# An mLSTM cell and a hash-routed expert layer on one core: moving two experts' weight loads to SyncE, a first layer into the attention block, and sums and turns into other gaps

## The chip, the core and the metric

The kernel runs on one core of a Trainium2 chip. A core has TensorE (matrix products into PSUM), VectorE, ScalarE and GpSimd (element work; GpSimd does not read PSUM here), and SyncE, which in this kernel only issues loads and stores. Loads and stores are also issued by ScalarE and, where rows are picked by an index, by GpSimd. Each engine works through its own list of instructions in order; semaphores tie the lists together.

The metric is the device time of one execution in microseconds. Before the change it is 373.84 us, the median of 3 runs (373.79 to 373.99).

## The reference, cut to what matters

Two blocks follow each other. The first is a recurrent attention cell over 4 batches, 8 heads and 768 positions, with heads of 40:

```python
for t in range(S):
    m_new = np.maximum(f_gate[:, :, t] + m, i_gate[:, :, t])
    f_stab = np.exp(f_gate[:, :, t] + m - m_new)
    i_stab = np.exp(i_gate[:, :, t] - m_new)
    m = m_new
    C = f_stab[:, :, None, None] * C + i_stab[:, :, None, None] * np.einsum('bhd,bhe->bhde', vt, kt)
    n = f_stab[:, :, None] * n + i_stab[:, :, None] * kt
    h_tilde = np.einsum('bhde,bhe->bhd', C, qt)
    denom = np.maximum(np.abs(np.einsum('bhd,bhd->bh', n, qt)[:, :, None]), 1.0)
    y[:, :, t] = o * h_tilde / denom          # o = sigmoid(o_gate[:, :, t])
```

Its output, laid out as 3072 rows of 320, is the input of the second block: eight experts, each a two-layer network with a ReLU. The expert of a row is a hash of its token id, so a row's expert is known from `token_ids` alone:

```python
expert_idx = token_ids * np.int64(2654435761) % np.int64(E)      # E = 8
for e in range(E):
    mask = expert_idx == e
    h = np.maximum(x[mask] @ w1[e], 0.0)                         # w1: 8 x 320 x 1024
    out[mask] = h @ w2[e]                                        # w2: 8 x 1024 x 320
```

Everything is float32. One expert's weights are 1.31 MB for `w1` and 1.31 MB for `w2`.

## The kernel before, in words

**Attention block.** The rows are cut into 24 tiles of 128 positions (`NT`), four batches by six stretches. A loop over s from 0 to 23 writes out by hand, instruction by instruction, the order of the work: the whole block stands in a manual schedule, so each engine executes in the order of the code, with small deviations. In step s TensorE turns the keys and queries of tile s+2 (`turn`, L332), forms the scores of tile s+1 (L380) and its decay matrices (L343, L351), and attends for tile s (L432, L438). VectorE weighs the scores (L386), divides (L447 to L451) and does small pieces of two side tasks: the gates' sums and splits (`Gates`, the object `g2` serves the last stretch), and the routing. GpSimd multiplies with the output gate (`gated`, L455), and SyncE stores the finished tile's rows to `x_rows` in DRAM (L458).

The routing turns token ids into two index tables: `g_idx` says which row of `x_rows` goes to which slot of which expert, `s_idx` where the result row goes. Its pieces are spread over the steps by the dictionaries `pieces` (VectorE and GpSimd) and `products` (TensorE, at a step's end): one-hot matrices in eight parts (`route_hot`), four table products (`route_table`), then `route_index` and `route_tiles`. The products' PSUM tiles bear the tag of the turns (`tr`, two banks).

During the last steps the weights of expert 0 come in slices over SyncE (`slices_of`), and two of its three full row tiles, whose rows all lie in the first 19 tiles, are gathered and turned (`early_turn`).

**Expert block.** An expert has three full tiles of 128 slots and a rest of 32 (`CAP` 416 slots); the rests of four experts make one further tile (`rest`, L1099). For experts 1 to 7 both layers use a seven-product scheme for 2x2 blocks (Strassen's, in Winograd's form): `layer1_by_seven` (L951, L959) needs sums of the rows (`sums_of_x`, L912 to L915, tile `tx`) and of the first weights (`sums_of_w1`, L905 to L908, tile `sw`); `layer2_by_seven` (L1022) needs sums of h and differences of the second weights. It works in two halves of 208 columns by two row-block pairs each: seven products into four PSUM banks, VectorE additions out of them (L937), ScalarE ReLUs. The banks of the first half are those of the second, so TensorE's second product of the second half waits for VectorE's addition out of the first half's second bank. The third full tile of each expert goes through plain `layer2` (L990). Results leave by a copy into `zo` (L835) and an indexed store (L839, GpSimd).

Rows come to an expert in four steps. `fetch(e)` lets GpSimd gather three tiles by `g_idx` (L110), and SyncE writes them to a DRAM buffer `x_slots` (L1068; the rests L1075). `blocks(e)` reads them back as twelve small loads into `xb`, with 32x32 blocks in place (L1083, SyncE). `turned(e)` turns the blocks in one VectorE instruction (L1087). Expert 0 is an exception: `layer1` first runs over its two early tiles (columns 0 to 256), then `layer2` over them, and the third tile and the rest are gathered and turned by TensorE in between (`turns0`, L852 to L858).

Weights of experts 1 and 2 are issued by ScalarE from inside expert 0's first `layer1` (the argument `between`): L97, L100 twice, L101. Those of expert e+3 are issued by SyncE at the end of expert e.

In the loop over e, expert e+2's rows are fetched, and expert e+1's are turned and summed, after expert e's `layer2` and before its `layer2_by_seven`:

```python
            layer2(W[e], h, (2,), cols_of(s_idx, e * NJ), True)
            if e + 1 < E:
                if e + 2 < E:
                    fetch(e + 2)
                    blocks(e + 2)
                turned(e + 1)
                sw = sums_of_w1(W[e + 1])
                tx = sums_of_x(xTs[e + 1])
            if i == EG - 1:
                rest(g)
            if e > 0:
                layer2_by_seven(W[e], tw, h, sh, cols_of(s_idx, e * NJ))
            if e + 3 < E:
                load_weights(e + 3)
```

**Semaphores of loads.** The framework gives the loads of SyncE and ScalarE eight completion semaphores in turn. Before a load is issued its engine waits until the previous load on the same semaphore has landed.

Of the kernel before, what the change touches and what calls it, by code (L numbers as in the profile page):

```python
# [17 lines left out]
P = 128  # L18
# [4 lines left out]
def kernel(  # L23
# [96 lines left out]
    def slices_of(e):  # L120
# [17 lines left out]

        return [lambda i=i: part(i) for i in range(7)]

    firsts = (0, 1, NB - 1, NB)
# [10 lines left out]
    with tc.tile_pool(name="gates", bufs=1) as gp, \  # L152
# [304 lines left out]
        def store(s):  # L457
            nc.sync.dma_start(x_d[s * P : (s + 1) * P, :], st.pop(s)["x"].rearrange("p h d -> p (h d)"))  # L458
# [52 lines left out]
        def route_turned():  # L511
            tp = ps.tile([P, NT], F32, name="tpe", tag="tr", bufs=2)
            nc.tensor.transpose(tp[:], et[:], ident[:NT, :NT])
            nc.vector.tensor_copy(ef[:], tp[:])
# [222 lines left out]
        for s in range(NT):  # L737
# [121 lines left out]

    def layer1(w, xT, h, c0, c1, between=lambda fp: None):  # L860

        w1t, w1c, _ = w
        for fp in range(FB // 2):
            hp = [mps.tile([P, CAP], F32, name="mh", bufs=4) for _ in range(2)]

            def halves(first):
                for i in range(2):
                    r = slice(i * P // 2, (i + 1) * P // 2)
                    nc.tensor.matmul(  # L869
                        hp[i][:, : c1 - c0], lhsT=w1c[r, fp, :], rhs=xT[r, 2, c0:c1], start=first, stop=not first,  # L870
                    )

            def whole(i, first):
                fb = 2 * fp + i
                for db in range(2):
                    nc.tensor.matmul(
                        hp[i][:, : c1 - c0], lhsT=w1t[:, db, fb * P : (fb + 1) * P], rhs=xT[:, db, c0:c1],
                        start=(first and db == 0), stop=(not first and db == 1),
                    )

            def out(i):
                if i == 0:
                    nc.vector.tensor_relu(h[:, 2 * fp, c0:c1], hp[i][:, : c1 - c0])
                else:
                    nc.scalar.activation(h[:, 2 * fp + 1, c0:c1], hp[i][:, : c1 - c0], AF.Relu)  # L885

            if fp % 2 == 0:
                for i in range(2):
                    whole(i, True)
                between(fp)  # L890
                halves(False)
                for i in range(2):
                    out(i)
            else:
                halves(True)
                for i in range(2):
                    whole(i, False)
                    out(i)
                between(fp)

# [30 lines left out]
    def layer1_by_seven(w, sw, xT, tx, h, done):  # L931

# [9 lines left out]
        for g in range(0, FB // 2, 2):  # L942
# [112 lines left out]
    with tc.manual_schedule():  # L1055
# [50 lines left out]
        fetch(1)  # L1106
        blocks(1)
        for e in range(E):
            g, i = e // EG, e % EG
            h = xp.tile([P, FB, CAP], F32, name="h", bufs=1) if e else h0  # L1110
            if i == 0:
                hrem[g] = xp.tile([P, EG, FB, RM], F32, name="hrem")

            if e == 0:
                layer1(W[0], xT0, h, 0, 2 * P, lambda fp: len(W) < 3 and load_weights(len(W), nc.scalar))
                layer2(W[0], h, range(2), cols_of(s_idx, 0), True, lambda j: j == 0 and turns0())
            if e == 0:
                layer1(W[e], xT0, h, 2 * P, CAP)
            else:
                tw = differences_of_w2(W[e])  # L1120
                sh = xp.tile([P, 4, FB // 2, P], F32, name="sh", bufs=1)
                layer1_by_seven(
                    W[e], sw, xTs[e], tx, h,
                    lambda g: sums_of_h(h, sh, g, nc.vector if g else nc.gpsimd),
                )
            nc.gpsimd.tensor_copy(hrem[g][:, i], h[:, :, NM:])
            layer2(W[e], h, (2,), cols_of(s_idx, e * NJ), True)
            if e + 1 < E:
                if e + 2 < E:
                    fetch(e + 2)  # L1130
                    blocks(e + 2)
                turned(e + 1)
                sw = sums_of_w1(W[e + 1])
                tx = sums_of_x(xTs[e + 1])
            if i == EG - 1:
                rest(g)
            if e > 0:
                layer2_by_seven(W[e], tw, h, sh, cols_of(s_idx, e * NJ))
            if e + 3 < E:
                load_weights(e + 3)  # L1140

    nx = nc.values_load(xe[0:1, NX : NX + 1], min_val=0, max_val=NX)
    with tc.If(nx > 0):
        with tc.For_i(0, nx, 1) as k:
# [9 lines left out]
            xT = xp.tile([P, DB, CAP], F32, name="xT")  # L1154
            h = xp.tile([P, FB, CAP], F32, name="h", bufs=1)
            gather(xr[:, :Dm], gs[:, 0:1])
            turn(xr, xT[:, :, :P], False)
            layer1(w, xT, h, 0, P)
            layer2(w, h, range(1), lambda j: gs[:, 1:2], False)

# [29 lines left out]
```

## Time and profile before

| | |
|---|---|
| median of 3 runs | 373.84 us |
| profiled execution, its own time | 374.24 us |
| its span, first to last instruction | 372.1 us |
| TensorE, VectorE, GpSimd, ScalarE busy | 93%, 58%, 56%, 37% of the span |
| mean granted TensorE clock | 0.984 |
| last product of attention ends, about | 132.4 us |
| layer one of expert 1 starts | 174.4 us |
| layer one of expert 2 starts | 201.3 us |

The profile is a record of one execution. Start times are microseconds from the span's start. PE is TensorE, DVE VectorE, ACT ScalarE, POOL GpSimd; SPq and ACTq are the loads that SyncE and ScalarE issue, with the time of the issue, not of the transfer. `x_slots<-xg` means that `x_slots` is written from `xg`. A tail in square brackets is how long the engine was idle before the instruction and what ended that. The view of waits sums such idle times by pair: total, times, longest. The chain is followed back from the last instruction, at each step to what released it. Numbers behind an L are lines of the kernel before.

### The profile page before, as it was taken

What the parts mean: (1) busy time and instruction counts of PE and PEld (TensorE: products, weight loads), DVE (VectorE), ACT (ScalarE), POOL (GpSimd) and SP (SyncE); (2) the same over time, 40 slices, a digit from 0 to 9 for tenths busy, and PEclk for the clock granted to TensorE, in tenths of its full rate; (3) what the DMA queues carried; (4) which work ended last, traced back from release to release, by engine and by line L of the source; (5) the groups of instructions that cost most, each with busy time, mean ns of one, the idle gap of its engine ahead of it and who ended that gap; (6) DMA issues with size and microseconds to landing.
All of it is one profiled execution on the core that took longest, in us unless ns stands there. A gap on an engine that the chain in (4) does not pass through costs nothing.

```text
span 372.1 us, 9193 instructions
## 1 busy us (share of the span) xinstructions
PE 344.4 (93%) x3595; PEld 295.1 (79%) x3595; DVE 215.4 (58%) x494; ACT 138.1 (37%) x311; POOL 206.9 (56%) x292
## 2 busy tenths in 40 slices
PE   7899899999999987399998999999999999999990
PEld 7777788878888764278988889859989899899680
DVE  7567787798779731017566483563483574755310
ACT  6476578666666530011320312301312313212210
POOL 8432668898883415021964936843936747419312
PEclk9999999999999999699999999999999999999997
DMA  7699989989898889560378695495945865200000
GB/s 145 120 182 174 185 164 197 211 173 202 171 201 221 212 259 333 191 132 3 124 161 281 140 303 147 83 296 166 235 139 153 199 192 135 36 18 35 9 11 36
DMA packets 163155, 59.35 MB, mean 159 GB/s; under 512 B 140130, under 2 KB 159102, under 8 KB 163110
## 3 DMA queue, kind: packets, MB, share of 16 engines
q1 hardware_dynamic: 155606, 44.97, 53.2%
q0 software_dynamic: 2496, 8.20, 7.1%
q10 hardware_dynamic: 5008, 5.57, 4.8%
q8 instruction: 29, 0.48, 0.5%
q14 instruction: 16, 0.13, 0.1%
HBM read 46.57 MB, written 12.48 MB: 159 GB/s over the span
## 4 chain that ended last, share of the span: by engine, by line
PE 75%; DVE 8%; DMA 7%; issue 4%; ACT 2%; POOL 2%; SPq 1%; ACTq 0%; DVEq 0%; POOLq 0%
PE mh L951 17%; PE mh L1022 11%; PE zp L990 10%; PE sp L380 7%; PE tr L332 6%; PE mh L959 5%; PE xh L438 4%; PE ab L343 3%; PE xh L432 3%; PE zp L1099 2%; PE xh L411 2%; DMA xr<-x_rows,g_idx 2%; DMA x_rows<-x 2%; SPq L1083 1%; DVE w L386 1%
## 5 line engine op out<-in xcount | busy, mean ns | idle before, releaser
L839 POOL DMA_INDIRECT out_dram<-zo,s_idx x26 | 26.2, 1006 | 83.3 <-ACT zo L835 49.0
L990 PE MATMUL zp<-w2t,h 128*128 128x320 f32 x160 | 46.7, 445 | 7.5 <-ACT h L885 7.5
L990 PEld LDWEIGHTS zp<-w2t,h 128*128 128x128 f32 x160 | 30.9, 196 | 19.5 <-ACT h L885 8.0
L937 DVE TENSOR_TENSOR h<-u,mh 128x416 f32<-128x416 f32 x42 | 24.6, 588 | 30.2 <-PE mh L959 13.9
L438 PE MATMUL xh<-v,w 128*64 128x41 f32 x768 | 34.9, 222 | 0.3 <-issue 0.3
L386 DVE TENSOR_TENSOR w<-sp,w 128x512 f32<-128x512 f32 x48 | 30.7, 682 | 4.8 <-ACT w L347 4.8
L347 ACT ACTIVATE w<-ab 128x512 f32<-128x512 f32 x48 | 26.1, 597 | 17.1 <-PE ab L343 17.0
L110 POOL DMA_INDIRECT xg<-x_rows,g_idx x24 | 24.5, 1019 | 14.0 <-PE mh L869 7.0
L951 PE MATMUL mh<-tx,sw 128*128 128x208 f32 x168 | 31.8, 339 | 0.0
L438 PEld LDWEIGHTS xh<-v,w 128*64 128x64 f32 x768 | 30.7, 138 | 0.4 <-issue 0.4
L380 PE MATMUL sp<-qT,kT 64*128 64x128 f32 x384 | 29.3, 285 | 1.5 <-DVE w L386 1.2
L951 PEld LDWEIGHTS mh<-tx,sw 128*128 128x128 f32 x168 | 29.7, 190 | 0.0
L380 PEld LDWEIGHTS sp<-qT,kT 64*128 64x128 f32 x384 | 24.3, 187 | 6.0 <-issue 2.3
L1022 PE MATMUL mh<-tw,sh 128*128 128x160 f32 x168 | 27.4, 299 | 0.0
L432 PE MATMUL xh<-C,qs 128*64 128x82 f32 x320 | 27.3, 249 | 0.0
L455 POOL TENSOR_TENSOR x<-x,og 128x320 f32<-128x320 f32 x24 | 20.6, 863 | 10.7 <-ACT og L372 6.9
L421 POOL TENSOR_TENSOR C<-C,add 64x164 f32<-64x164 f32 x32 | 16.3, 509 | 14.8 <-ACT add L415 13.6
L1022 PEld LDWEIGHTS mh<-tw,sh 128*128 128x128 f32 x168 | 24.3, 190 | 0.0
L951 PE MATMUL mh<-xT,w1t 128*128 128x208 f32 x112 | 24.3, 339 | 0.0
L937 DVE TENSOR_TENSOR u<-m,mh 128x416 f32<-128x416 f32 x28 | 15.9, 587 | 14.2 <-ACT m L965 7.1
L959 PE MATMUL mh<-xT,w1c 64*128 64x208 f32 x224 | 23.5, 349 | 0.0
L974 ACT ACTIVATE h<-mh 128x416 f32<-128x416 f32 x14 | 7.2, 517 | 42.6 <-PE mh L959 39.3
(236 smaller groups left out, 744.5 us busy)
## 6 DMA issues: line engine op xcount, KB each, us to landing
w2t<-in_moe_w_dram SPq DMA_DIRECT2D x5, 1280.0 KB
w1t<-in_moe_w_dram SPq DMA_DIRECT2D x5, 1024.0 KB
xb<-x_slots SPq DMA_DIRECT2D x84, 52.0 KB
k<-in_k_dram SPq DMA_DIRECT2D x24, 160.0 KB
v<-in_v_dram SPq DMA_DIRECT2D x24, 160.0 KB
og<-in_o_gate_dram SPq DMA_DIRECT2D x24, 160.0 KB
x_rows<-x SPq DMA_DIRECT2D x24, 160.0 KB
q<-in_q_dram SPq DMA_DIRECT2D x23, 160.0 KB
```

The costliest lines, as they stand in the source:

```text
L110: nc.gpsimd.indirect_dma_start(out=xg, out_offset=None, in_=x_d[:rows, :], in_offset=bass.IndirectOffsetOnAxis(ap=idx, axis=0),)
L347: nc.scalar.activation(w[:, hf], ab[:], AF.Exp)
L380: nc.tensor.matmul(sp[hf][:, j, :], lhsT=d["kT"][r, j, :], rhs=d["qT"][r, j, :], start=True, stop=True)
L386: nc.vector.tensor_tensor(d["w"][:, hf], d["sp"][hf][:], d["w"][:, hf], op=ALU.mult)
L432: nc.tensor.matmul(xh[t, 2 * j : 2 * j + 2, :], lhsT=d["qs"][:, j, t], rhs=Cs[b][c % 2][:, j].rearrange("p h d -> p (h d)"), start=True, s ...
L438: nc.tensor.matmul(hs[t, 2 * j + hf, :], lhsT=d["w"][:, hf, j, t], rhs=d["v"][:, 2 * j + hf, :], start=(c == 0), stop=True, skip_group_che ...
L839: ins = nc.gpsimd.indirect_dma_start(out=out[:, :], out_offset=bass.IndirectOffsetOnAxis(ap=idx, axis=0), in_=zo[:], in_offset=None, bound ...
L937: nc.vector.tensor_tensor(o, a, b, op=ALU.add)
L951: nc.tensor.matmul(pair(bank[n])[:, a], lhsT=lhsT(g + a), rhs=rhs, start=first and a == 0, stop=True, skip_group_check=True,)
L959: nc.tensor.matmul(pair(bank[n])[:, a], lhsT=w1c[k, g + a, :], rhs=xT[k, 2, r], start=False, stop=True, skip_group_check=True,)
L990: nc.tensor.matmul(zp[:], lhsT=h[:, fb, j * P : (j + 1) * P], rhs=w[2][:, fb, :], start=(fb == 0), stop=(fb == FB - 1),)
L1022: nc.tensor.matmul(bank[n], lhsT=lhsT(f), rhs=rhs(f), start=first and f == 0, stop=f == FB // 2 - 1, skip_group_check=True,)
```

## The change

The change has these parts.

1. **Weights of experts 1 and 2.** ScalarE no longer issues them. SyncE does, after expert 1's `fetch` and `blocks` and before expert 2's.
2. **First layer's first part.** `layer1` is moved up and takes its PSUM banks as an argument. Its run over expert 0's first 256 columns now stands at the end of the attention block, on banks of the turns and decays (`tr`, `ab`).
3. **Fetch.** `fetch(e + 2)` and `blocks(e + 2)` stand at the head of expert e.
4. **Turns and sums.** `turned(e + 1)` is called inside expert e's `layer1_by_seven`, in the first half, behind its first three VectorE additions, and `sums_of_x` likewise in the second half (`meanwhile`). For expert 1 both stand after expert 0's second `layer1`. `tx` gets two buffers. `sums_of_w1` stays.
5. **h.** All experts use the one buffer `h0`.
6. **Last rest.** `rest` of the second group goes behind the last `layer2_by_seven`.
7. **Attention's side tasks.** `g2.ends` and the `e` split go from step 10 to 8; the one-hot parts and tables one step later (12 to 19), `route_index` to 20 and `route_tiles` to 21; the routing's PSUM tiles take the scores' banks (`sp0`, `sp1`).

```diff
-            tp = ps.tile([P, NT], F32, name="tpe", tag="tr", bufs=2)
+            tp = ps.tile([P, NT], F32, name="tpe", tag="sp0")
...
-            cps = ps.tile([P, 2, E, NT], F32, name="cps", tag="tr", bufs=2)
+            cps = ps.tile([P, 2, E, NT], F32, name="cps", tag="sp1")
...
-            tk = ps.tile([P, 2, NC], F32, name="tk", tag="tr", bufs=2)
+            tk = ps.tile([P, 2, NC], F32, name="tk", tag="sp0")
...
-            19: [route_index], 20: [route_tiles],
+            20: [route_index], 21: [route_tiles],
...
-            pieces.setdefault(11 + i, []).append(lambda i=i: route_hot(i))
+            pieces.setdefault(12 + i, []).append(lambda i=i: route_hot(i))
             if i % 2:
-                products[11 + i] = [lambda i=i // 2: route_table(i)]
+                products[12 + i] = [lambda i=i // 2: route_table(i)]
...
-            if s == 10:
+            if s == 8:
                 g2.ends()
                 g2.split("e")
...
+        layer1(W[0], xT0, h0, 0, 2 * P, lambda i: ps.tile([P, 4 * P], F32, name="mh0", tag=("tr", "ab")[i], bufs=2))
...
-        tx = xp.tile([P, 4, HC], F32, name="tx", bufs=1)
+        tx = xp.tile([P, 4, HC], F32, name="tx")
...
             add(v[:], v[:], bank[3][:])
+            meanwhile(g)
             product(0, lambda fp: block(fp, 0, 1), xT[:, 1, lo])
...
         blocks(1)
+        for e in (1, 2):
+            load_weights(e)
+        h = h0
         for e in range(E):
             g, i = e // EG, e % EG
-            h = xp.tile([P, FB, CAP], F32, name="h", bufs=1) if e else h0
+            if e + 2 < E:
+                fetch(e + 2)
+                blocks(e + 2)
...
             if e == 0:
-                layer1(W[0], xT0, h, 0, 2 * P, lambda fp: len(W) < 3 and load_weights(len(W), nc.scalar))
                 layer2(W[0], h, range(2), cols_of(s_idx, 0), True, lambda j: j == 0 and turns0())
-            if e == 0:
-                layer1(W[e], xT0, h, 2 * P, CAP)
+                layer1(W[0], xT0, h, 2 * P, CAP, bank)
+                turned(1)
+                tx = sums_of_x(xTs[1])
             else:
                 tw = differences_of_w2(W[e])
                 sh = xp.tile([P, 4, FB // 2, P], F32, name="sh", bufs=1)
+                txs = [tx]
+
+                def meanwhile(g):
+                    if e + 1 < E:
+                        if g == 0:
+                            turned(e + 1)
+                        else:
+                            txs.append(sums_of_x(xTs[e + 1]))
+
                 layer1_by_seven(
-                    W[e], sw, xTs[e], tx, h,
+                    W[e], sw, xTs[e], tx, h, meanwhile,
                     lambda g: sums_of_h(h, sh, g, nc.vector if g else nc.gpsimd),
                 )
+                tx = txs[-1]
...
             if e + 1 < E:
-                if e + 2 < E:
-                    fetch(e + 2)
-                    blocks(e + 2)
-                turned(e + 1)
                 sw = sums_of_w1(W[e + 1])
-                tx = sums_of_x(xTs[e + 1])
-            if i == EG - 1:
+            if i == EG - 1 and e + 1 < E:
                 rest(g)
             if e > 0:
                 layer2_by_seven(W[e], tw, h, sh, cols_of(s_idx, e * NJ))
+            if e + 1 == E:
+                rest(g)
```

More of the change, by code (lines that the diff above doesn't have):

```diff
@@ L139, in slices_of, with layer1, halves, whole @@
         return [lambda i=i: part(i) for i in range(7)]
+    def layer1(w, xT, h, c0, c1, bank):
+        w1t, w1c, _ = w
+        for fp in range(FB // 2):
+            hp = [bank(i) for i in range(2)]
+            def halves(first):
+                for i in range(2):
+                    r = slice(i * P // 2, (i + 1) * P // 2)
+                    nc.tensor.matmul(
+                        hp[i][:, : c1 - c0], lhsT=w1c[r, fp, :], rhs=xT[r, 2, c0:c1], start=first, stop=not first,
+                    )
+            def whole(i, first):
+                fb = 2 * fp + i
+                for db in range(2):
+                    nc.tensor.matmul(
+                        hp[i][:, : c1 - c0], lhsT=w1t[:, db, fb * P : (fb + 1) * P], rhs=xT[:, db, c0:c1],
+                        start=(first and db == 0), stop=(not first and db == 1),
+                    )
+            def out(i):
+                if i == 0:
+                    nc.vector.tensor_relu(h[:, 2 * fp, c0:c1], hp[i][:, : c1 - c0])
+                else:
+                    nc.scalar.activation(h[:, 2 * fp + 1, c0:c1], hp[i][:, : c1 - c0], AF.Relu)
+            if fp % 2 == 0:
+                for i in range(2):
+                    whole(i, True)
+                halves(False)
+                for i in range(2):
+                    out(i)
+            else:
+                halves(True)
+                for i in range(2):
+                    whole(i, False)
+                    out(i)
     firsts = (0, 1, NB - 1, NB)
@@ L858, in turn, with bank @@
             nc.vector.tensor_copy(dst, tp[:])
[L860 to L899, printed above, removed]
+    def bank(i):
+        return mps.tile([P, CAP], F32, name="mh", bufs=4)
     HC, HD = CAP // 2, Dm // 2
@@ L929, in sums_of_x, with layer1_by_seven @@
         return tx
-    def layer1_by_seven(w, sw, xT, tx, h, done):
+    def layer1_by_seven(w, sw, xT, tx, h, meanwhile, done):
         w1t, w1c, _ = w
@@ L1121 @@
                 sh = xp.tile([P, 4, FB // 2, P], F32, name="sh", bufs=1)
+                txs = [tx]
[3 more added lines that the diff above has]
+                            turned(e + 1)
+                        else:
+                            txs.append(sums_of_x(xTs[e + 1]))
                 layer1_by_seven(
-                    W[e], sw, xTs[e], tx, h,
+                    W[e], sw, xTs[e], tx, h, meanwhile,
                     lambda g: sums_of_h(h, sh, g, nc.vector if g else nc.gpsimd),
                 )
+                tx = txs[-1]
             nc.gpsimd.tensor_copy(hrem[g][:, i], h[:, :, NM:])
@@ L1154 @@
             xT = xp.tile([P, DB, CAP], F32, name="xT")
-            h = xp.tile([P, FB, CAP], F32, name="h", bufs=1)
             gather(xr[:, :Dm], gs[:, 0:1])
             turn(xr, xT[:, :, :P], False)
-            layer1(w, xT, h, 0, P)
-            layer2(w, h, range(1), lambda j: gs[:, 1:2], False)
+            layer1(w, xT, h0, 0, P, bank)
+            layer2(w, h0, range(1), lambda j: gs[:, 1:2], False)
 _INS = ['q', 'k', 'v', 'i_gate', 'f_gate', 'o_gate', 'moe_token_ids', 'moe_w1', 'moe_w2']
```

## The prediction

> All times are on the clock of the profiled execution before: span 372.1 us, its own time 374.24, so 2.1 lie around the span; the median of the runs is 373.84, 0.4 lower. A difference worked out on the span is applied to the median. About 0.2% (0.75 us) is what a measurement of this kernel can tell from no change.
>
> **What bounds the kernel now.** First the page: busy shares and the chain that ended last.
>
> ```profile
> PE 344.4 (93%) x3595; PEld 295.1 (79%) x3595; DVE 215.4 (58%) x494; ACT 138.1 (37%) x311; POOL 206.9 (56%) x292
> PE 75%; DVE 8%; DMA 7%; issue 4%; ACT 2%; POOL 2%; SPq 1%; ACTq 0%; DVEq 0%; POOLq 0%
> ```
>
> TensorE is the bound, and the chain leaves it for 25%. From 201 us on TensorE is packed: one expert is 13.45 (by seven, layer one) + 4.31 + 7.61 (by seven, layer two) = 25.4 us, repeated. So only the stretch between attention's last tile (132 us) and 201 us, attention's own steps and the tail can change. The view of waits names the largest stall, the timeline shows its cause:
>
> ```profile
> ACT h L885 <- DMA x_slots<-xr: 14.8, 1, 14.8
> PE zp L990 <- ACT h L885: 7.5, 1, 7.5
> ```
>
> ```profile
> 153.59 0.38 ACTq L101 DMA_DIRECT2D w2t<-in_moe_w_dram  x1
> 154.44 0.50 PEld L990 LDWEIGHTS zp<-w2t,h 128*128 128x128 f32 x2 [8.01 <-ACT h L885]
> ```
>
> ScalarE issues the third expert's last load (L101) between two of its ReLUs. In the program eight completion semaphores go round the loads of SyncE and ScalarE, and a load waits until the last user of its semaphore has landed. This one's was SyncE's x_slots<-xr, so ScalarE stood until 153.59 with two ReLUs queued behind the load, and TensorE stood from 146.9 to 154.4. Then the chain, in order of time (start, us, what):
>
> ```profile
> 134.69 6.12 DMA x_rows<-x
> ...
> 142.94 6.51 DMA xr<-x_rows,g_idx
> 149.65 3.92 DMA x_slots<-xr
> ...
> 179.25 2.90 DMA xg<-x_rows,g_idx
> 182.27 2.78 DMA x_slots<-xg
> ...
> 190.58 2.06 DMA xb<-x_slots
> 192.77 1.48 DVE xT L1087
> ```
>
> The last store and the gather behind it run beside two experts' weights (6.12 and 6.51 us); at 179 a gather without such company takes 2.90. Expert 2's rows (gather, x_slots in DRAM, twelve xb, turn) make the second half of the chain: TensorE lost 1.46 us at it (from 187.88, the start of expert 1's layer two, to 201.26, the start of expert 2, less 4.31 + 7.61). SyncE's own timeline gives this row path's prices where nothing disturbs it:
>
> ```profile
> 203.66 0.37 SPq L1068 DMA_DIRECT2D x_slots<-xg  x1
> 206.53 6.01 SPq L1083 DMA_DIRECT2D xb<-x_slots  x12
> 212.65 0.41 SPq L97 DMA_DIRECT2D w1t<-in_moe_w_dram  x1
> ```
>
> The xb issues start 2.87 after the x_slots issue (2.81 to 2.87 elsewhere) and take 6.0 for twelve.
>
> **What the Trainium skill says.** "DMA: Bandwidth & Descriptors", section "Issuing engines are not separate DMA queues": loads started from several engines share the same 16 DMA engines; moving a load saves only sequencer time. The trace agrees: both queues fill to 380-410 GB/s. Its section "Queues, rings and completion order": each DMA engine takes one issuer's descriptors in ring order. No run here shows it yet; my likeliest case rests on it. "TensorE: Matmul & The Clock Gate", section "What's actually happening": after an idle window of about 3.4 us the clock halves, and needs as much busy time to return. Here it halved 4.7 us after TensorE stopped and came back 4.0 us after it restarted (151.7 and 158.5), so a long stall costs another 2.0 us.
>
> **The change, part by part.**
>
> *Attention.* The `e` split moves from step 10 to 8, the one-hot pieces from 11-18 to 12-19, so VectorE's pile at 70 to 75 us goes. The steps there, from one first transpose to the next, took 5.03 and 5.63 us where a plain one takes 4.83, a loss of 1.0, of which I take 0.9; step 9, where the split now falls, had 1.75 of VectorE idle. The four tables leave the transposes' banks for those of the scores: the step behind a table took 5.01, so 0.18 four times, 0.7. The index (ten operations, 2.1 us) now falls in step 20, whose TensorE work is 4.37 against 5.5 on VectorE: cost 0.6 of the 1.1, as later steps absorb some. Bounds +0.5 and -1.8; I take **-1.0**.
>
> *First layer's first part inside the block.* It starts when xT0 is copied (132.65) instead of at 133.78, with no loads between ScalarE's ReLUs. 32 passes at 0.217 (208 columns take 0.176) + 16 x 0.148 = 9.3: ends 142.0. Then 0.6 for the last ReLU, 4.31 (layer two, rows 0), 1.5 (turns), 4.31, 6.1 (second part, 163.88 to 169.98), 4.31: layer one by seven of expert 1 starts at 163.1 instead of 174.42, **11.3 us earlier**. This needs expert 1's w1t by then, which it has, below. But this gain is kept only if nothing further on waits.
>
> *Rows and weights on SyncE.* Removed from ScalarE: 8 loads. Added to SyncE: the same 8, behind x_slots(1) and twelve xb(1), and ahead of x_slots(2) and twelve xb(2). With no weights beside it, the last store lands in about 2.4 us (6.12 with; a 480 KB x_slots takes 2.8): 137.1. First gather 137.75 (0.65 later, as at 140.94 to 141.64), the fifth 4 x 1.26 after: 142.8. Gather to x_slots issue 3.02 (279.75 to 282.76): 145.8. x_slots to xb 2.84: 148.65. Twelve xb issues 6.1: 154.8. Weights: first bytes 1.95 after issue (212.65, 214.6): 156.7. One expert's 2.62 MB with a scatter took 214.5 to 222.0; without it 7.1; with three gathers 2.1 more. Two experts, three gathers (expert 3's, now issued at about 164) and one scatter: 16.7: done 173.4. w1t of expert 1 (1.05 MB, 2.8, and a receipt) lands near 160.5, early enough. x_slots(2) was issued at 160 but lies behind both experts in the ring: 0.49 MB and its receipt, 1.9: **175.3**. Twelve xb(2) 6.1, landing 1.7: **183.1** (192.77 before).
>
> On GpSimd the three gathers of expert 2 go ahead of the first scatter and of the copy into xT0: its eight gathers end at 147.6, the first scatter is ready at 147.6, so nothing waits.
>
> *Turns and sums in the gaps.* The turn of expert e+1 now stands on VectorE between the third addition of layer one's first half and its additions into h; the sums stand in the second half. In the steady state that costs nothing that TensorE sees (on VectorE they take 1.48 and 1.4): the turn ends 5.3 us after the half's start, and TensorE wants the addition behind it at 7.6. Cover gone at expert 1: VectorE stands at the turn for xb(2), behind it the additions into h that free the banks, and for these TensorE's second product of the second half. TensorE gets there at 163.1 + 6.73 + 0.87 = 170.7 and resumes at 183.1 + 1.48 + 0.59 + 0.2 = 185.4: a **14.7 us stall**. The rest of the half is 5.86, and 2.0 for the clock: 193.3, against 187.88. **+5.4.** From there VectorE no longer has turn and sums before layer two's additions: **-1.46** at expert 1 and **-0.25** at expert 3.
>
> *Fetch at the loop's head.* Expert 3's gathers come early; its xb lands near 199, wanted by 207: hidden, margin 8 us. Later ones have about 10. One buffer h instead of two: by its first write layer two of expert 0 is done.
>
> *Tail.* `rest` of the second group moves behind the last layer two, so TensorE's end stays but one scatter follows instead of two. Before: scatters at 364.19 and 365.48, end 372.1. After: product ends 363.2, copy, scatter 0.7 later, 363.94: **-1.54**.
>
> Sum: -1.0 + 5.4 - 1.46 - 0.25 - 1.54 = **+1.15**: span 373.25, median **375.0**.
>
> **Rivals.** *A, ring order is not what holds x_slots(2).* If its write passes the weights, the seventh xb(2) still waits for the semaphore of expert 2's w2t: 173.4 + 6 x 0.5 + 1.7 = 178.1, 5.0 earlier: 370.0. It decides as soon as xb(2) lands before 181.9, where the sum is zero: weights at the 395 GB/s seen for single microseconds go the same way. For: the issue is at 160. Against: both are on one queue. *B, transfers slower:* from 134 to 148 two experts' loads beside gathers averaged 330 GB/s; 5.9 MB take 17.9, 1.2 more, a late store 0.5, and twelve xb took 7.3 twice, 1.2 more: 377.9. *C, hidden anyway:* no stall at expert 1 at all, 176.6 instead of 193.3: 358.3. The wait stands in the program's order and 5 MB cannot be there by 170; hardly possible. *D, the gaps are not gaps:* if turn and sums held TensorE up 0.5 us in each of six experts: 378.0; in the profile VectorE has idle of 1.0 before those additions, against it.
>
> **How the numbers follow.** Likeliest 0.50, own range 373.5 to 376.5; A 0.22, B 0.20, C 0.04, D 0.04. The range 370.9 to 379.0 leaves out C, half of A's early end and the late ends of B and D. Faster: A's 0.20, C 0.04, 0.03 of the likeliest: 0.27. Same: 0.14 of the likeliest and 0.02 of A. Slower: 0.57.
>
> **What would show it.** TensorE idle near 171 to 185, then half clock for 4 us; the VectorE turn waiting for xb<-x_slots by over 10 us; ScalarE's 14.8 us wait gone; layer one by seven starting near 162; the last scatter near 363.9 plus what the sum moved. The prediction is wrong if the turn waits under 10 us, or if w1t of expert 1 comes after 163.

## The result, and the profile after

The changed kernel takes **383.59 us** (median of 4, 382.79 to 383.77), the kernel before 373.91 beside it (373.79 to 374.49): a ratio of 1.0252, interval 1.0233 to 1.0270. The prediction said 375.0 (370.9 to 379.0). Slower was right, but the loss is 9.7 us and not 1.15. Line numbers are now those of the kernel after: L939 additions, L953 and L961 layer one by seven, L993 plain layer two, L1025 layer two by seven, L1071 `x_slots`, L1086 `xb`, L1090 the turn, L914 to L917 differences (`tx` on VectorE, `tw` on GpSimd), L907 to L910 sums (`sw`, `sh`).

The page of the kernel after, busy shares and the shares of the chain that ended last:

```profile
PE 344.0 (90%) x3595; PEld 295.9 (77%) x3595; DVE 230.8 (60%) x494; ACT 137.3 (36%) x311; POOL 208.8 (55%) x292
PE 62%; DVE 12%; DMA 8%; issue 5%; SPq 4%; ACT 4%; POOL 2%; POOLq 0%; ACTq 0%; DVEq 0%
```

TensorE's share of the chain fell from 75% to 62%, VectorE's rose from 8% to 12%. VectorE is busy 15.4 us longer (230.8 against 215.4) with the same 494 instructions: some of them became slower, and 15.0 of the 15.4 us are in the subtractions for `tx` shown below. TensorE's waits (total, times, longest):

```profile
PE mh L953 <- DVE h L939: 16.8, 1, 16.8
PE zp L993 <- ACT h L983: 3.5, 4, 1.8
PE tpx L719 <- DMA xg<-x_rows,g_idx: 1.9, 1, 1.9
```

ScalarE's 14.8 us wait for `x_slots<-xr`, and TensorE's 7.5 behind it, are gone as forecast. The first line is the forecast stall of expert 1. The other two were not forecast. The stall, in the timeline (start, length, what, idle time before it):

```profile
169.50 0.87 PE L953 MATMUL mh<-xT,w1t 128*128 128x208 f32 x4
185.13 1.48 DVE L1090 STREAM_TRANSPOSE xT<-xb 128x1248 f32<-128x1248 f32 x1 [18.76 <-DMA xb<-x_slots]
186.54 1.54 DVE L939 TENSOR_TENSOR h<-u,mh 128x416 f32<-128x416 f32 x3
187.14 3.14 PE L953 MATMUL mh<-tx,sw 128*128 128x208 f32 x8 [16.77 <-DVE h L939]
```

VectorE stands at expert 2's turn for 18.8 us; the additions into h behind it free TensorE's banks. SyncE's timeline of the kernel after shows why the rows are late:

```profile
149.28 6.07 SPq L1086 DMA_DIRECT2D xb<-x_slots  x12
155.39 0.47 SPq L97 DMA_DIRECT2D w1t<-in_moe_w_dram  x1
...
161.74 4.86 SPq L1071 DMA_DIRECT2D x_slots<-xg  x1
177.37 6.01 SPq L1086 DMA_DIRECT2D xb<-x_slots  x12
```

Expert 2's `x_slots` follows eight weight loads. Its issue alone took 4.86 us (0.39 for the one at 145.51), and it landed at 177.35, 15.61 us after its issue began. The second line of the waits comes from here, expert 2's layer one, second half, GpSimd and VectorE in one timeline:

```profile
217.85 1.54 POOL L915 TENSOR_TENSOR tw<-w2t,tw 128x640 f32<-128x640 f32 x1
217.98 1.64 DVE L914 TENSOR_TENSOR tx<-xT 128x208 f32<-128x208 f32 x1
...
219.35 1.67 POOL L916 TENSOR_TENSOR tw<-w2t 128x640 f32<-128x640 f32 x1
219.66 1.60 DVE L915 TENSOR_TENSOR tx<-xT,tx 128x208 f32<-128x208 f32 x1
220.98 1.67 POOL L917 TENSOR_TENSOR tw<-w2t,tw 128x640 f32<-128x640 f32 x1
221.18 1.70 DVE L916 TENSOR_TENSOR tx<-xT 128x208 f32<-128x208 f32 x1
```

VectorE's subtractions for `tx` took 0.37 us each in the kernel before; two of its lines, under its own line numbers:

```profile
221.44 0.37 DVE L912 TENSOR_TENSOR tx<-xT 128x208 f32<-128x208 f32 x1
221.84 0.38 DVE L913 TENSOR_TENSOR tx<-xT,tx 128x208 f32<-128x208 f32 x1
```

In the kernel after, each takes about as long as one of GpSimd's differences of W2 and ends 0.23 us after the one that was running when it began (219.62 and 219.39 for the first). The fourth, beside GpSimd's sums of h, takes 0.89. At experts 3 to 5 the four take 4.6 us together, at expert 6 2.9, where before they took 1.5. The spans by stretch, on each kernel's own clock:

| stretch | before | after | difference | forecast |
|---|---|---|---|---|
| start to layer one of expert 1 | 174.42 | 162.77 | -11.65 | -12.3 |
| layer one of expert 1 | 13.46 | 33.05 | +19.59 | +16.7 |
| rest of expert 1 | 13.38 | 11.92 | -1.46 | -1.46 |
| experts 2 to 6 | 131.90 | 136.07 | +4.17 | -0.25 |
| expert 7 and the end | 38.94 | 38.09 | -0.85 | -1.54 |
| sum | 372.1 | 381.9 | +9.8 | +1.15 |

Two rows hold most of the 8.65 us between forecast and result: 4.4 in experts 2 to 6, 2.9 in the stall.

### The profile page after: what moved, and what is told of

The parts are those of the page before. It is cut to its first block, busy times and chain, and to the rows that moved or that the text cites. A ratio compares the mean times of both kernels' runs of the same rounds, so it can differ in the third digit from the quotient of the medians.

```text
span 381.9 us, 9195 instructions
## 1 busy us (share of the span) xinstructions
PE 344.0 (90%) x3595; PEld 295.9 (77%) x3595; DVE 230.8 (60%) x494; ACT 137.3 (36%) x311; POOL 208.8 (55%) x292
## 4 chain that ended last, share of the span: by engine, by line
PE 62%; DVE 12%; DMA 8%; issue 5%; SPq 4%; ACT 4%; POOL 2%; POOLq 0%; ACTq 0%; DVEq 0%
PE mh L953 16%; PE mh L1025 12%; PE zp L993 6%; PE sp L419 5%; DMA x_slots<-xg 5%; PE tr L371 5%; PE mh L961 4%; PE xh L477 4%; SPq L1086 3%; PE ab L382 3%; DMA xg<-x_rows,g_idx 2%; PE xh L471 2%; PE xh L450 2%; DVE tx L916 2%; DVE tx L915 2%
## 5 line engine op out<-in xcount | busy, mean ns | idle before, releaser
L879 POOL DMA_INDIRECT out_dram<-zo,s_idx x26 | 27.4, 1056 | 83.0 <-issue 46.5
L993 PE MATMUL zp<-w2t,h 128*128 128x320 f32 x160 | 45.9, 436 | 4.0 <-ACT h L983 3.5
L953 PE MATMUL mh<-tx,sw 128*128 128x208 f32 x168 | 34.1, 355 | 16.8 <-DVE h L939 16.8
L953 PEld LDWEIGHTS mh<-tx,sw 128*128 128x128 f32 x168 | 31.4, 200 | 17.3 <-DVE h L939 17.1
L993 PEld LDWEIGHTS zp<-w2t,h 128*128 128x128 f32 x160 | 29.8, 190 | 16.9 <-ACT h L983 5.5
L425 DVE TENSOR_TENSOR w<-sp,w 128x512 f32<-128x512 f32 x48 | 30.7, 681 | 5.3 <-ACT w L386 5.3
L110 POOL DMA_INDIRECT xg<-x_rows,g_idx x24 | 23.4, 976 | 12.6 <-issue 6.7
L939 DVE TENSOR_TENSOR h<-u,mh 128x416 f32<-128x416 f32 x42 | 23.3, 576 | 10.0 <-PE mh L953 6.7
L1025 PE MATMUL mh<-tw,sh 128*128 128x160 f32 x168 | 27.4, 299 | 0.0
L494 POOL TENSOR_TENSOR x<-x,og 128x320 f32<-128x320 f32 x24 | 20.6, 866 | 9.6 <-ACT og L411 7.3
L939 DVE TENSOR_TENSOR u<-m,mh 128x416 f32<-128x416 f32 x28 | 16.0, 588 | 15.4 <-PE mh L953 7.9
L953 PE MATMUL mh<-xT,w1t 128*128 128x208 f32 x112 | 24.7, 344 | 0.0
L1025 PEld LDWEIGHTS mh<-tw,sh 128*128 128x128 f32 x168 | 24.3, 190 | 0.0
L961 PE MATMUL mh<-xT,w1c 64*128 64x208 f32 x224 | 23.5, 349 | 0.0
```

The lines of the kernel that those rows point to most:

```text
L110: nc.gpsimd.indirect_dma_start(out=xg, out_offset=None, in_=x_d[:rows, :], in_offset=bass.IndirectOffsetOnAxis(ap=idx, axis=0),)
L425: nc.vector.tensor_tensor(d["w"][:, hf], d["sp"][hf][:], d["w"][:, hf], op=ALU.mult)
L879: ins = nc.gpsimd.indirect_dma_start(out=out[:, :], out_offset=bass.IndirectOffsetOnAxis(ap=idx, axis=0), in_=zo[:], in_offset=None, bound ...
L939: nc.vector.tensor_tensor(o, a, b, op=ALU.add)
L953: nc.tensor.matmul(pair(bank[n])[:, a], lhsT=lhsT(g + a), rhs=rhs, start=first and a == 0, stop=True, skip_group_check=True,)
L961: nc.tensor.matmul(pair(bank[n])[:, a], lhsT=w1c[k, g + a, :], rhs=xT[k, 2, r], start=False, stop=True, skip_group_check=True,)
```

## The experiments

Theory 1: the stall of expert 1 comes from the order of SyncE's issues. Theory 2: experts 2 to 5 lose because VectorE's subtractions run beside GpSimd's. An expert's period is the time from the start of its layer one to that of the next expert's; in the kernel after the periods of experts 2 to 6 are 27.45, 30.86, 26.20, 26.19 and 25.37 us, and 25.37 is the packed one (30.01 at expert 3, with the first group's remainder product). The rivals: the rows are late whatever the order; turn and sums are too much work for the gaps (the prediction's D). Unless said otherwise each kernel is the one after with the edit shown; ratios are to the kernel before.

### SyncE's order

`order`:

```diff
         fetch(1)
+        fetch(2)
         blocks(1)
-        for e in (1, 2):
-            load_weights(e)
+        load_weights(1)
+        blocks(2)
+        load_weights(2)
...
-            if e + 2 < E:
+            if e and e + 2 < E:
```

> The kernel after with one thing changed, the order of SyncE's issues: x_slots(1), x_slots(2), twelve xb(1), expert 1's weights, twelve xb(2), expert 2's weights. Theory 1 (expert 2's rows stand behind both experts' weights in SyncE's queue, and that alone makes the stall at expert 1): TensorE's 16.8 us wait for h in expert 1's second half is gone, x_slots(2) is issued near 150, xb(2) lands near 166, layer one by seven of expert 1 ends near 176.5 instead of 196.0, time 363 to 368. Rival (rows are late for another reason, gathers or the sharing of the DMA engines): the stall shrinks by under 5 us, 379 to 383. Second rival (expert 2's weights, now last, become the next thing to be late): rows come by 166 but layer one of expert 2 waits for w1t(2); time 368 to 375.

Measured: 371.84 us, ratio 0.9952 (0.9935 to 0.9970), span 370.7, 11.2 less than after. The stall shrank to 7.4 us and did not go; the time is within the second rival's range, but not by its mechanism, since no product waits for `w1t`. SyncE's timeline of `order`:

```profile
156.15 0.60 SPq L101 DMA_DIRECT2D w2t<-in_moe_w_dram  x1
156.80 13.08 SPq L1086 DMA_DIRECT2D xb<-x_slots  x12
```

Twelve `xb` issues take 6.0 us at 177.37 in the kernel after and 13.1 here, right behind one expert's weights. My expectation had left out that expert 1's weights still stood ahead of `xb(2)`. The next run puts these weights ahead of all rows, so that they are through before the rows come: `w1first`, with the guard of the loop's fetch as above.

```diff
+        load_weights(1)
         fetch(0)
         fetch(1)
+        fetch(2)
         blocks(1)
-        for e in (1, 2):
-            load_weights(e)
+        blocks(2)
+        load_weights(2)
```

> The kernel after with one thing changed, SyncE's order again: expert 1's weights right behind the last store of attention, then the rows of experts 0, 1 and 2, twelve xb(1), twelve xb(2), expert 2's weights last. In the run with the order rows, weights 1, xb(2), weights 2 the turn of expert 2 still waited 9.4 us, and its twelve xb issues took 13.1 us behind expert 1's weights where twelve take 6.0 elsewhere. Theory 1 (each transfer of rows is late by the weights that stand ahead of it in SyncE's queue, and by nothing else): with no weights ahead of xb(2) twelve issues take 6 to 7 us, the turn of expert 2 waits for the third addition and no longer for xb, expert 1's layer one by seven takes under 15 us (23.6 and 33.2 before), span 370.7 less 9 to 10, time 361 to 364. Rival (rows are late by the gathers or by the DMA engines' load, whatever the order): the turn still waits over 5 us, time 368 to 372.

Measured: 367.60 us, ratio 0.9824 (0.9798 to 0.9850), span 366.3. Expert 1's layer one takes 13.46 us (166.58 to 180.04), as in the kernel before. Expert 1's weights are issued from 131.63 to 135.28, before any row, and expert 2's behind the rows; nothing stands between the rows any more. All 24 `xb` issues take 12.39 us, and the turn of expert 2 no longer waits:

```profile
152.42 12.39 SPq L1086 DMA_DIRECT2D xb<-x_slots  x24
170.10 1.47 DVE L1090 STREAM_TRANSPOSE xT<-xb 128x1248 f32<-128x1248 f32 x1
```

The stall is gone. **Theory 1 stands.** The time is 3.6 above its range because that layer starts at 166.58 instead of 161.28. What was late next: attention's last store now went out behind `w1t`, the first gather at 138.18 instead of 134.91, a gathered tile's copy on VectorE waited for it until 143.54 ahead of expert 0's last ReLU, and TensorE stood 2.96 us and ran its next 16 products in 6.23 instead of 4.47.

`oldturn` undoes the place of turn and sums from expert 1 on, and leaves SyncE's order as in the kernel after:

```diff
-                    W[e], sw, xTs[e], tx, h, meanwhile,
+                    W[e], sw, xTs[e], tx, h, lambda g: None,
...
-                tx = txs[-1]
...
             if e + 1 < E:
+                if e:
+                    turned(e + 1)
                 sw = sums_of_w1(W[e + 1])
+                if e:
+                    tx = sums_of_x(xTs[e + 1])
```

> The kernel after with one part undone: from expert 1 on, the turn and the sums of x of the next expert stand again behind the middle rows of layer two, where the kernel before has them; SyncE's order and all else as after. Theory 1 with 2 (the loss comes from what stands on VectorE behind a late xb(2), and from sums beside GpSimd's differences): layer one of expert 1 runs through (13.6 us, end near 176.4 instead of 196.0), the wait for xb(2), still landing near 185, moves into layer two by seven of expert 1: turn, sums of W1 and of x end near 191, expert 2 starts near 195.5 instead of 207.7; the periods of experts 2 to 5 go back to 25.4, 4.6 us; span 364 to 366, time 365.5 to 368. Rival (the place of the turn doesn't matter, the rows are late in any case): 379 to 384.

Measured: 372.36 us, ratio 0.9953 (0.9929 to 0.9977), span 370.7. Layer one of expert 1 runs through (163.15 to 176.60), and the turn, still late, holds up layer two instead. The lines are from the views of VectorE's timeline and of TensorE's waits:

```profile
187.00 1.48 DVE L1090 STREAM_TRANSPOSE xT<-xb 128x1248 f32<-128x1248 f32 x1 [7.38 <-DMA xb<-x_slots]
```

```profile
PE mh L1025 <- DVE u L1039: 6.7, 1, 6.7
```

Expert 2 starts at 197.07, 10.7 us earlier than after. So the late rows cost far more because the turn stands ahead of layer one's additions than where it stood before. The run missed its range by 4 us: the periods of experts 2 to 5 are 27.5, 30.7, 26.0 and 26.0, not 25.4, although the subtractions are at 0.37. At expert 3 VectorE's addition out of the first half's third bank starts 6.86 us after the layer's start instead of 6.23, the next one 8.30 instead of 6.93, both waiting for TensorE. The products that they need start as elsewhere (6.02 and 6.73), but the trace's semaphore events have TensorE's signals at 6.83 and 8.28, where `fixed`, below, has them at 6.21 and 6.91. `best`, below, has the same at experts 2 to 5, with the very code that `fixed` has there, so the place of turn and sums doesn't cause it. It shows at the experts with gathers on GpSimd and in these two runs alone, which ran on another chip than `order`, `w1first`, `tx0`, `tx_apart`, `both` and `fixed`. The cause stays open.

### Sums beside GpSimd's differences

`tx0` puts all sums into the first half:

```diff
                         if g == 0:
                             turned(e + 1)
-                        else:
                             txs.append(sums_of_x(xTs[e + 1]))
```

> The kernel after with one thing changed: the sums of x of the next expert follow its turn in the first half of layer one, where GpSimd has gathers and no sums, instead of standing in the second half, where GpSimd makes the differences of W2. Theory 2 (VectorE's subtractions with two SBUF inputs are slowed from 0.37 to 1.6 us because GpSimd's run beside them): the four take 0.37 each again, the experts' periods from 2 on go from 27.5, 30.9, 26.2, 26.2 back to about 25.5, 30.4, 25.4, 25.4, time 379 to 380. Rival (turn and sums are simply too much work ahead of the additions into h, wherever they stand): four subtractions at 0.37, but the first half is held up instead, time 383 to 386.

Measured: 386.99 us, ratio 1.0339 (1.0280 to 1.0398), span 384.6; the range of theory 2 is missed, and the rival's by 1. But at experts 2 to 5 the subtractions are at 0.37 and the periods at 25.37, 30.01 (with the remainder), 25.37 and 25.37: 4.6 us off. What takes the gain away is expert 6, 5.2 us longer. GpSimd has nothing to gather there, so its differences come in the first half. VectorE's timeline of `tx0` at expert 6:

```profile
319.51 1.47 DVE L1090 STREAM_TRANSPOSE xT<-xb 128x1248 f32<-128x1248 f32 x1
321.02 1.75 DVE L914 TENSOR_TENSOR tx<-xT 128x208 f32<-128x208 f32 x1
322.80 1.59 DVE L915 TENSOR_TENSOR tx<-xT,tx 128x208 f32<-128x208 f32 x1
324.31 1.70 DVE L916 TENSOR_TENSOR tx<-xT 128x208 f32<-128x208 f32 x1
325.93 0.36 DVE L917 TENSOR_TENSOR tx<-xT,tx 128x208 f32<-128x208 f32 x1
```

GpSimd's differences begin at 319.35, 320.99, 322.49 and 324.12 and end at 325.8. The turn, which reads one tensor, keeps its 1.47 beside them; the subtractions, which read two, do not; the fourth, after GpSimd's end, is at 0.36 again. The rest of the loss is ahead of expert 2: a start 1.4 later, and 0.8 for sums now behind the late turn. `tx_apart` keeps the two apart everywhere:

```diff
                         if g == 0:
                             turned(e + 1)
-                        else:
+                        if (g == 0) == (1 < e < E - 2):
                             txs.append(sums_of_x(xTs[e + 1]))
```

> The kernel after with one thing changed: the sums of x stand where GpSimd makes no differences of W2, that is in the first half at experts 2 to 5 and in the second half at experts 1 and 6. At 6 no gathers stand ahead of the differences on GpSimd, so they fall in the first half, and in the run with all sums in the first half the slow subtractions moved there (1.75, 1.59, 1.70 us) and TensorE lost 5.2 us at expert 6. Theory 2 (the subtractions are slow only where GpSimd's differences run beside them): all of them at 0.37, every period from 2 to 6 at 25.4 (29.9 with the remainder), 4.6 us off, time 378.5 to 379.5. Rival (VectorE's work in the gaps is too much in either half): 382 to 387.

Measured: 378.31 us, ratio 1.0131 (1.0094 to 1.0169), span 375.9. All periods from 2 to 6 are 25.37 (30.01 with the remainder). VectorE and GpSimd at expert 2:

```profile
211.34 0.37 DVE L914 TENSOR_TENSOR tx<-xT 128x208 f32<-128x208 f32 x1
...
212.32 0.37 DVE L917 TENSOR_TENSOR tx<-xT,tx 128x208 f32<-128x208 f32 x1
...
214.79 1.56 POOL L914 TENSOR_TENSOR tw<-w2t 128x640 f32<-128x640 f32 x1
```

At expert 6 three of the four still take 0.78 to 0.90, beside GpSimd's sums of h, and TensorE loses nothing to that. The same turn and sums inside layer one cost nothing when they stand clear of GpSimd's differences: **theory 2 stands, and the rival, too much work, falls.**

`tw_copy` asks what on GpSimd does it:

```diff
-        differences(*b, [tw[:, i] for i in range(4)], nc.gpsimd)
+        for i in range(4):
+            nc.gpsimd.tensor_copy(tw[:, i], b[i])
```

> The kernel after with GpSimd's four differences of W2 per expert replaced by four copies of the same size (the differences of W2 are left out of the computation, so layer two by seven is not what the reference asks for). GpSimd then reads one SBUF input instead of two, VectorE's subtractions still two. If any GpSimd work on SBUF holds up a VectorE instruction with two SBUF inputs: the subtractions beside the copies still take over 1 us. If it takes two inputs on both sides: 0.37 each, and about 4 us off the span of 381.9. If GpSimd's work has nothing to do with it: 1.6 as before.

Measured: one run at 379.15, span 377.4, 4.5 less. The copies take about 0.7 us each instead of 1.55 and are soon over, so that only at expert 2 two subtractions stand beside them; the others stand beside GpSimd's sums of h, at up to 0.90:

```profile
216.19 2.88 POOL L1006 COPY tw<-w2t 128x640 f32<-128x640 f32 x4
218.03 0.46 DVE L914 TENSOR_TENSOR tx<-xT 128x208 f32<-128x208 f32 x1
218.53 0.78 DVE L915 TENSOR_TENSOR tx<-xT,tx 128x208 f32<-128x208 f32 x1
```

The second ends at 219.31, 0.24 us after the last copy (219.07), as the subtractions above end 0.23 after GpSimd's differences. So copies seem to hold VectorE up too, until they end; that they read one tensor isn't enough to free it. With two subtractions, and neither the first case's 1 us nor the second's 0.37, this is thin.

### Both mended

`both` joins `order` and `tx0`:

> Both edits, the order of SyncE's issues and the sums of x in the first half. If the two causes are independent the gains add: about 19 and 4 us off 383.6, time 359 to 364. If they share a cause or something else is late next, less: 365 to 370.

Measured: 374.15 us, ratio 1.0005 (0.9988 to 1.0022), outside either range: the remaining 7.1 us stall with the sums now behind it, expert 6's 5.2, and a wait of 1.8 for a gather in attention that `order` did not have. `fixed` joins `w1first` and `tx_apart`:

> Both edits of the two runs before, the order with expert 1's weights first and the sums of x apart from GpSimd's differences. If the two causes of the loss are these and independent: 361 to 364 less 4.6, time 356 to 360, under the kernel before by 14 and more. If something else is late next: 361 to 368.

Measured: **362.98 us**, ratio 0.9708 (0.9667 to 0.9750), span 361.1. It beats the kernel before by 11 us and the one after by 20.6. It is 4.6 below `w1first`: the causes add. The first range is missed by 3 for what was late next in `w1first`. `best` tried to mend that; its edit is shown against `fixed`:

```diff
-        load_weights(1)
         fetch(0)
+        load_weights(1)
...
-                        if (g == 0) == (1 < e < E - 2):
+                        if (g == 0) == (e < E - 2):
```

> The run with both mendings, with expert 1's weights one place later in SyncE's order, behind the store of expert 0's remainder rows instead of ahead of the gathers, and the sums of expert 2 in the first half too. In that run the last store of attention went out between the first weights and the first gather came 2.9 us later than in the run where the rows went first; a gathered tile's copy on VectorE then held back the last ReLU, and TensorE lost 2.7 us and 1.8 more at half clock. If this is all: 357 to 359.5. If expert 1's rows, now behind its weights, are late instead: layer one by seven of expert 1 starts after 165, 360 to 364.

Measured: 378.04 us, ratio 1.0103 (1.0065 to 1.0141), beyond both ranges. Now expert 1's own rows stand behind its weights: `xb(1)` is issued from 158.08 instead of 152.02 in `fixed`. VectorE's timeline of `best`:

```profile
165.85 1.48 DVE L1090 STREAM_TRANSPOSE xT<-xb 128x1248 f32<-128x1248 f32 x1 [6.39 <-DMA xb<-x_slots]
...
168.63 0.69 DVE L907 TENSOR_TENSOR sw<-w1t 128x512 f32<-128x512 f32 x1
169.23 2.43 DVE L908 TENSOR_TENSOR sw<-w1t 128x512 f32<-128x512 f32 x1
171.70 1.91 DVE L909 TENSOR_TENSOR sw<-sw,w1t 128x512 f32<-128x512 f32 x1
173.64 1.91 DVE L910 TENSOR_TENSOR sw<-w1t,sw 128x512 f32<-128x512 f32 x1
```

At expert 1 TensorE waits 3.4 us for the turn and 5.3 for the sums of W1. These slid into GpSimd's differences, which start at 169.56 whether rows have come or not, and took 1.9 to 2.4 instead of 0.69. Both theories in one stretch: a late transfer moved VectorE's work to where GpSimd held it up. That isn't the whole loss: of the 13.8 us between the spans of `fixed` and `best`, 4.4 lie at experts 2 to 5, from TensorE's late signals that `oldturn` has too and that nothing here explains.

### Attention and the tail

`side` is the kernel before with part 7 of the change alone:

> The kernel before with only attention's own edits: tables in the scores' banks, the split at step 8, one-hot pieces, index and tiles a step later. The prediction's term, -1.0, gives 372.9. If the later index also makes the first early turn wait for its gather (1.95 us in the kernel after), the gain is eaten: 373.5 to 375. If attention gains 1.6 and more and nothing waits: under 372.3.

Measured: 371.80 us, ratio 0.9938 (0.9919 to 0.9957): -2.3 by the ratio, twice the forecast term; the third case holds. No early turn waits for its gather. `side_noshift` leaves out the shift by one step (the edit is shown against `side`):

```diff
-            20: [route_index], 21: [route_tiles],
+            19: [route_index], 20: [route_tiles],
...
-            pieces.setdefault(12 + i, []).append(lambda i=i: route_hot(i))
+            pieces.setdefault(11 + i, []).append(lambda i=i: route_hot(i))
...
-                products[12 + i] = [lambda i=i // 2: route_table(i)]
+                products[11 + i] = [lambda i=i // 2: route_table(i)]
```

> The kernel before with attention's edits but for the shift: tables in the scores' banks and the split at step 8, the one-hot pieces, index and tiles in their old steps. The run with the shift took 371.8, 0.9938 of before. If the later index costs 0.6 as the prediction has it, this one is faster than that by 0.3 to 0.6: 371.2 to 371.5. If the shift is what takes VectorE's pile away at 70 to 75 us, it is slower: 372.3 to 373.

Measured: 372.28 us beside a before of 374.34, ratio 0.9939 (0.9920 to 0.9958): the same gain, just short of the second case's range. The shift neither costs nor brings anything that shows. (The profiled execution, the slowest of the four, has a 1.7 us wait of an early turn for its gather, so that wait doesn't need the shift.)

TensorE's transposes show which edit pays. In the kernel before, the second half of step 5's transposes waits after the first routing product has taken one of their banks; in `side` step 9, the one behind the split, has a new wait:

```profile
39.90 0.66 PE L332 MATMUL tr<-ident,q 128*128 128x128 f32 x4 [0.68 <-ACT kT L333]
```

```profile
62.68 0.67 PE L411 MATMUL xh<-v,kw 128*64 128x41 f32 x16 [0.75 <-POOL gr L580]
```

From one first transpose to the next, step 5 takes 5.12 us in `side` instead of 5.90, step 6 5.52 instead of 5.67, and the four steps behind a table 4.79 instead of 5.29, 5.10, 5.10 and 5.10: 2.4 us, from the banks (0.2 of it, at the first table, may belong to the split). The split's move brings little or nothing: the loss of 1.0 at 69 to 80 us goes, and step 9 takes 5.80 instead of 4.83. `side_noshift` has the same steps. `tail` is the kernel before with part 6 alone:

> The kernel before with only the second group's remainder product moved behind the last layer two. The prediction's term, -1.54, gives a ratio of 0.9959. By the kernel after, where 8.1 us lie between TensorE's end and the span's end instead of 8.8, -0.65: ratio 0.998 to 0.9985.

Measured: 373.49 us, ratio 0.9978 (0.9963 to 0.9993). That is -0.8 us; -0.65 is inside, -1.54 (0.9959) outside the interval. The last scatter in this run's timeline:

```profile
363.99 0.99 POOL L839 DMA_INDIRECT out_dram<-zo,s_idx  x1 [2.11 <-ACT zo L835]
```

It is issued at 363.99, where the prediction had 363.94 (365.48 before), but from there to the span's end are 7.3 us instead of 6.6.

## Why the prediction was wrong

**Bound, gain up front, stall's place: right.** Layer one of expert 1 started at 162.77 (forecast 162.1), the turn waited 18.8 us, TensorE stood from 170.4 to 187.1, and expert 1's layer two got its 1.46 back. Rival A falls: `x_slots(2)` did not pass the weights, it landed 15.61 us after its issue began. The prediction took from the Trainium skill ("DMA: Bandwidth & Descriptors", "Queues, rings and completion order") that each DMA engine takes one issuer's descriptors in ring order. Three orders of the same loads agree: expert 2's turn waited 18.8 us with both experts' weights ahead of its rows, 9.4 with one's, and not at all in `w1first`.

**The failed step: "In the steady state that costs nothing that TensorE sees (on VectorE they take 1.48 and 1.4)".** It took the durations from a place where GpSimd was at other work, and asked what VectorE had to do in the new place, not what GpSimd did. The turn does take 1.48. The sums took 5.8 at expert 2 (1.64, 1.60, 1.70, 0.89) and 4.6 at experts 3 to 5, since part 3 of the change puts the gathers (four at expert 2) ahead of the differences of W2 on GpSimd: at expert 2 they run 8.5 to 14.9 us after layer one's start instead of 3.4 to 9.6. Experts 2 to 6 came out at +4.17 instead of -0.25, half of the error. Rival D had the place, not the cause, and its size, 3.0 in all, was short; the idle of 1.0 held against it was measured with fast sums. The skill names the cause: "GPSIMD Engine Reference", "1. Specifications", says that GpSimd's SBUF interfaces are shared with VectorE, with contention for VectorE instructions with two SBUF inputs. The runs agree, and add the price: 1.6 to 1.75 us instead of 0.37.

**Mis-sized: the stall, +16.7, measured +19.6.** In the term's own chain, gather to `x_slots` issue took 4.4, not 3.02, with three more gathers queued behind; `x_slots` to `xb` 3.8, not 2.84; eight weight issues 6.2 where 5.2 lay between 154.8 and 160; and `x_slots(2)` landed at 177.35 where 175.3 less attention's 1.0 was forecast. Each was priced from a place with less traffic beside it.

**Mis-sized: attention and tail.** -1.0 for attention was -2.3 in `side`, and its parts were off: -0.9 for the split was about nothing, -0.7 for the banks was -2.2 to -2.4 (a step behind a table took 5.10, not 5.01, and the two earlier products' banks were left out), and +0.6 for the index doesn't show. In the kernel after 1.9 went to the wait for an early gather, issued at 123.41 where `order`, with the same attention code, has 122.31. The store that SyncE issued ahead of it went out at 122.25 and 120.82; what held SyncE up differs from run to run, and was not settled. The tail's -1.54 was -0.85 (38.94 to 38.09 us from expert 7's start), because the time behind the last scatter is not a constant.

## What to carry to other kernels

When an instruction moves, look at what every engine does in the new place: a duration measured beside GpSimd's gathers is no price beside its element work. Before a wait moves ahead of work that frees another engine's buffers, ask whether its data can be late, and what stands ahead of that data in its queue. With both answered, the same change with another order of issues and another place for the sums gave -2.9% instead of +2.5%.

## What the runs showed of the hardware

- A VectorE subtraction of two SBUF tensors took 0.37 us alone and 1.6 to 1.75 beside GpSimd's operations of 1.55 us (two SBUF inputs): it ended 0.23 us after the GpSimd operation that was running when it began, so about one got through per GpSimd operation. VectorE additions with one input in PSUM kept 0.59, a turn with one input 1.47.
- An idle of 3.3 us was enough for TensorE's clock to halve, after work had resumed. In `both` TensorE stood from 312.8 to 316.07; by windows of 1 us (length, TensorE busy and its products, granted clock, share of the DMA engines, GB/s) the clock was full until 317 and then

```profile
317.00:318.00 1.00, 1.00 (x6) 0.61 0.00 0
318.00:319.00 1.00, 1.00 (x5) 0.50 0.00 0
```

so it fell about 4.4 us after the stop (4.7 in the kernel before), and the layer lost 1.9 us more than the wait of 3.3 (5.2 in all).

- SyncE's issues took longer right behind weights: an `x_slots` 4.86 us instead of 0.37, twelve `xb` 13.1 instead of 6.0.
